# Long convolution and phase mixing on one core: reversed order of the operand blocks in SBUF, yt stores on SP, and steps, W loads and filter copies in other places

## The chip, the core and the metric

The kernel runs on one core of a Trainium2 chip, as one launch. Its time is the device time of one execution in microseconds (us). Several executions are made and the median is given. The engines are named as in the profile: PE (matmul), PEld (weight load of PE), DVE (vector engine), ACT (activation engine), POOL (GpSimd, which also issues DMAs), SP (which only issues DMAs).

## The reference

With batch 8, sequence S = 5696 and 128 channels, a causal convolution over the sequence with a filter as long as the sequence comes first, then a mixing layer over the tokens:

```python
y = irfft(rfft(x, n=2*S, axis=1) * rfft(h, n=2*S, axis=0)[None], n=2*S, axis=1)[:, :S]   # x: 8 x S x 128
theta = y @ w_theta                                  # 128 x 128
zr, zi = y * cos(theta), y * sin(theta)
v = einsum('ts,bsd->btd', w_tok_r, zr) + einsum('ts,bsd->btd', w_tok_i, zi)   # two S x S matrices
u = y + v
out = u + maximum(u @ w_ch, 0)                       # float32
```

The two S x S matrices (W below) are float32 in DRAM and most of the arithmetic is their product with zr and zi.

## The kernel before

**The convolution** is a Fourier transform made of matmuls, in eight groups: four pairs of batches (`bp`) by two halves of the channels (`dh`). Each group has four stages. `stage_a` transforms along one index of the split sequence. `stage_b` does the second transform (`f2`) and multiplies by the filter's transform, whose pieces are loaded as tiles `hs`, four of them at a time (`LEAD`); the product goes to the tile `uv_t`. `stage_c` transforms back from `uv_t` to a tile `g`, and `stage_d` from `g` to the tile `yt` with tables `e_t`. `yt` is stored to DRAM as `yt_hbm`. Stages of neighbouring groups are woven together by `woven`, which sorts their steps by a position between two bounds.

The filter's transform of the first group is taken from SBUF (`hs<-a`, line 421), and written to DRAM (`h_store`, line 369) for the other groups. `swap_rows` (lines 401 to 406) then copies it within DRAM, real and imaginary part swapped, to the second half of the rows; the loads of `hs` for the other groups (line 423) read both.

**The phase steps.** `phase_step(ti, hh)` takes 128 tokens of one half of the batches (`hh`), transposes them on PE, forms theta, sine and cosine on ACT and zr and zi on DVE in one tile `zz`, and stores y as `y2_hbm` (line 756) and `zz` as `z_hbm` (line 620) or straight into an operand block (line 616). y lies in one of six slots of 512 columns in the last three of the seven parts of block b0. `zz` is one of seven tiles taken in turn: index 0 to 3 from the pool of the `hs` tiles, 4 to 6 from a pool of its own; the counter is `zz_n`. The 22 steps of `hh` = 0 (`steps0`) need y of the first four batches. Three run ahead of the last group's stages, nine are woven into its stage c, five into its stage d, and five come behind. The 22 steps of `hh` = 1 (`steps1`) follow: two alone, twenty between the first products of the mixing (`next_steps`). Their y2 stores and half of their stores into the blocks go through POOL. Their last input, the row of the last `yt`, is copied into `ya` on POOL (line 729), and `sides["row"]` is that copy: the stores of `yt` from token H = 2816 on (line 502) are ordered behind it on POOL.

**The mixing.** The products are made for blocks of W of 3 times 64 columns, transposed by DVE (line 894), against eleven operand blocks b0 to b10 of z, each 14,336 bytes on each partition. b0 lies in the same tile as the ring of W. b1 to b6 are allocated where the convolution's tiles were, as soon as that is closed, in the order of their loads (`tile_b`, `load_b_half`); `load_b_half` loads the part that the `steps0` made from `z_hbm` and the `steps1` write the rest directly. b7 and b8 follow during `steps1`, b9 and b10 (line 817) when these are done, in a pool that lies over the tiles of `ya` and `hs`. The first stretch of products (`i == 1`) runs in four quarters `q`: halves `h` of the batches by sub-blocks `s`; the quarters with `h` = 1 need the parts that `steps1` write.

**W loads.** The W pieces are loaded on POOL with conversion to bf16, four DMAs to a piece (line 680), into a ring of six slots. `pump` issues as many as `ring["upto"]` allows and as slots are free. Before, six are released within stage c of the last group (`with_load`), two in the second quarter of the first stretch, the rest behind it. Later W pieces are released as their slots are read.

**Order.** Up to the first group's end DVE, ACT and POOL keep the order of the program text; later a scheduler orders each engine's instructions by the text and by estimated readiness, and `tc.issue_after(i)` asks that instructions on `i`'s queue come behind `i`. SP is always so scheduled. Every engine executes its instructions in order, and an instruction that waits holds up all behind it.

Of the kernel before, what the change touches and what calls it, by code (L numbers as in the profile page):

```python
# [22 lines left out]
def kernel(  # L23
# [10 lines left out]
    nc = tc.nc  # L34
# [46 lines left out]
    HD = D // 2  # L81
# [306 lines left out]
    def e_table(n):  # L388
# [9 lines left out]
            cosine(e_t[:K1, n0:n0 + 11, 0, :], k3)  # L398
        return curves

    def swap_rows():
        for c0, c1, w in ((0, NCK // 2, HD * CK), (NCK // 2, NCK - 1, HD * CK), (NCK - 1, NCK, HD * CHK[-1][1])):
            for ri in range(2):
                dst, src = (hf_hbm[c0:c1, :, r0:r0 + 64, r, :w].rearrange("c h p n -> (c h) p n")
                            for r0, r in ((64, ri), (0, 1 - ri)))
                nc.sync.dma_start(dst, src)

    def e_minus():
        nc.vector.tensor_scalar(e_neg[:K1], e_t[:K1, 1:2 * NP:2], -1.0, None, op0=mult)
# [1 line left out]
    def stage_b(a_st, dh, warm=WARM, first=False):  # L411

        hs_of = {}

        def load(c):
            if c >= NCK:
                return
            hs = hs_of[c] = fh.tile([P, 2, HD * CK], F16, tag="hs", name="hs")
            w = HD * CHK[c][1]
            for e in range(2 if first else 0):  # L420
                nc.sync.dma_start(hs[64 * e:64 * e + 64, 1, :w], hst_of(c)[64 - 64 * e:128 - 64 * e, dh])
            if not first:
                nc.sync.dma_start(hs[:, :, :w], hf_hbm[c, dh, :, :, :w])

        def chunk(c):
            c0, ck = CHK[c]
            hv = hs_of[c][:, :, :HD * ck].rearrange("p r (d k) -> p r d k", k=ck)
            straight = hst_of(c)[:, dh].rearrange("p (d k) -> p d k", k=ck).unsqueeze(1) if first else hv[:, 0:1]
            ps = f2(a_st, c, warm)
            xs = fs.tile([P, 2, HD, CK], F16, tag="xs", name="xs")  # L430
            nc.scalar.activation(xs[:, :, :, :ck], ps, AF.Copy)  # L431
            if ck == CK and not first:
                nc.vector.tensor_tensor(  # L433
                    uv[:, :, :, c0:c0 + ck],
                    xs.rearrange("p e d k -> p e (d k)").unsqueeze(1).to_broadcast([P, 2, 2, HD * CK]),
                    hv.rearrange("p r d k -> p r (d k)").unsqueeze(2).to_broadcast([P, 2, 2, HD * CK]), op=mult)
            for r in range(2 if ck < CK or first else 0):
                nc.vector.tensor_tensor(  # L438
                    uv[:, 2 * r:2 * r + 2, :, c0:c0 + ck], xs[:, :, :, :ck],
                    (hv[:, 1:2] if r else straight).to_broadcast([P, 2, HD, ck]), op=mult)  # L440
            load(c + LEAD)
        return [lambda c=c: load(c) for c in range(LEAD)], [lambda c=c: chunk(c) for c in range(NCK)]
# [35 lines left out]
    def stage_d(st, bp, dh, then=None):  # L478
        def chunk(n0, cn):
            if n0 == 0:  # L480
                st["yt"] = fy.tile([P, NB, N2], BF16, tag="yt", name="yt")
            g_, yt = st["g"], st["yt"]
            ps = psum()
            nq = 5 if cn == CN else cn
            for j in range(cn):
                o = ps[:, j // nq, (j % nq) * NB:(j % nq + 1) * NB]
                terms = terms_of(n0 + j)
                for i, (at, e_) in enumerate(terms):
                    nc.tensor.matmul(o, g_[:K1, at, :], e_, start=(i == 0), stop=(i == len(terms) - 1))
            y_out = yt[:, :, n0:n0 + cn].rearrange("p m (a q) -> p m a q", q=nq)  # L490
            y_in = ps[:, :cn // nq, :nq * NB].rearrange("p a (q m) -> p m a q", q=nq)
            if n0 in (0, 3 * CN):
                nc.vector.tensor_copy(y_out, y_in)
            else:
                nc.scalar.activation(y_out, y_in, AF.Copy)
            if n0 + cn == N2:
                if then is not None:
                    then(yt)
                for t0, t1 in [(H, S)] if then else YP:
                    for e in range(2):  # L500
                        with tc.issue_after(sides["row"]) if then else ExitStack():
                            (nc.gpsimd if then else nc.sync).dma_start(
                                yt_hbm[dh * HD:(dh + 1) * HD, 2 * bp + e, t0:t1],
                                yt[64 * e:64 * e + 64].rearrange("p m n -> p (m n)")[:, t0:t1])
        return [lambda n0=n0, cn=cn: chunk(n0, cn) for n0, cn in CHN]

    zz_n, ZB = [0], 3
    groups = [(bp, dh) for bp in range(B // 2) for dh in range(2)]

    def front(g, by_dve=(), a_=None, spare=None):  # L510
# [176 lines left out]
    sides = {"phases": None}  # L687
# [46 lines left out]
    home_of = {}  # L734
# [41 lines left out]
    for g, (bp, dh) in enumerate(groups):  # L776
# [3 lines left out]
        if last:  # L780
            for _ in range(3):
                steps0.pop(0)()
        now = ([with_load(steps0.pop(0), n < 6) for n in range(9)] if last else [], 0.0, 0.88)
        c_ = stage_c(st, last)
        if g == 0:
            ec = []
# [7 lines left out]
        if g + 2 == len(groups):  # L794
            xin.close()
            open_phases()
            load_ya0()
        now = [steps0.pop(0) for _ in range(5)] if last else []
        woven((b_, 0.0, 0.8), (stage_d(st, bp, dh, load_ya1 if last else None), 0.08 if b_ else 0.0, 1.1 if b_ else 1.0), now)
        if g + 2 == len(groups):  # L800
            load_ya1(st["yt"], True)
# [1 line left out]
    conv.close()  # L803

    bpe = [ctx.enter_context(tc.tile_pool(name="bpool_e", bufs=1, side="right", reuse_waits="tile"))]
    bts_of = {0: [], 1: []}

    def tile_b(p, j, pool):
        t_ = ring["all"][:, WB:WB + BT] if j == 0 else pool.tile([P, BT], BF16, tag=f"b{j}", name=f"b{j}")
        bt = [t_[:, k * 1024:(k + 1) * 1024].rearrange("p (r n) -> p r n", r=2) for k in range(7)]  # L810
        bts_of[p].append(bt)
        return t_

    def load_b(p, j, pool, eng=nc.scalar):
# [8 lines left out]

    def load_b_half(j):

        t_ = home_of[j] = tile_b(0, j, home_pool(j))
        for z in range(2):
            with tc.issue_after(sides["row"]) if j else ExitStack():
                d_ = nc.gpsimd.dma_start(t_[:, z * 2048:z * 2048 + 1024],
                                         z_hbm[0, j, 0, z].rearrange("i (s r) n -> (i s) (r n)", r=2)).ins  # L830
            sides["row"] = d_ if j else sides["row"]

    def sum_ops(bt):
        b11, b12, b21, b22 = (bt[q] for q in (M2, M6, M7, M5))
# [8 lines left out]
    def sum_some(n):  # L843

        for o in [o for o in owed if o[1] <= 2 or done["used"] > o[0]][:n]:
            owed.remove(o)
            o[2]()

    for j in range(7):
        load_b_half(j)  # L850
    for step in steps0:
        step()
# [273 lines left out]
    for i, (k, p, tt, j0, s0, nj) in enumerate(stretches):  # L1126
# [101 lines left out]
        if i == 1:  # L1228
            for q, (h, s) in enumerate(((0, 0), (0, 1), (1, 0), (1, 1))):
                for n in range(4):  # L1230
                    for j in range(TJ):
                        product((held, a)[s], s * TJ + j, j, n, (h,))
                        if (n * TJ + j) % 2:
                            next_steps(1)
                    if n % 2 and q == 1:
                        ring["upto"] += 1
                        pump()
                    if q == 3 and n == 0:
                        nxt = prepare(2)
# [126 lines left out]
```

## Time and profile before

| | |
|---|---|
| median of 3 executions | 2036.03 us (2028.82 to 2040.0) |
| the profiled execution | 2039.61 us, its span 2037.8 us |
| busy in the span | PE 95%, PEld 53%, DVE 75%, ACT 31%, POOL 47% |
| mean granted clock of PE | 0.985 |
| DMA through POOL's queue | 157.47 MB, 60.7% of 16 engines' time |
| DMA through SP's queue | 163.03 MB, 27.4% |
| convolution, about | 0 to 385 us |
| phase steps, about | 331 to 444 us |
| mixing, about | 394 to 2037 us |

The profile is one execution, recorded instruction by instruction. Busy time is the time in which an engine has an instruction under way; the DMA share is the busy share of the core's 16 DMA engines, and some rows of it are over 1. The granted clock is the part of PE's full clock that it ran at. Who ended a wait is inferred from the semaphores, and where several were waited for the one that came last is named. Times in the views are in us from the start of the span.

### The profile page before, as it was taken

How to read it: one execution, taken by the hardware profiler on the slowest of the kernel's cores; microseconds unless marked ns; L12 is line 12 of the kernel's file. 1: busy time of each engine (PE TensorE's matmuls, PEld its weight loads, DVE VectorE, ACT ScalarE, POOL GpSimd, SP SyncE). 2: the span in 40 equal slices, each digit the busy share in tenths (PEclk: the TensorE clock that was granted, in tenths of full speed). 3: DMA queues.
4: the chain of work that ended last, by engine and by line, in shares of the span. 5: the costliest groups of instructions: out<-in, count | busy, mean ns of one | idle time of the engine just before them, and what ended most of it. 6: DMA issues, size and time to landing. Idle time of an engine off the chain costs nothing.

```text
span 2037.8 us, 42414 instructions
## 1 busy us (share of the span) xinstructions
PE 1945.8 (95%) x16121; PEld 1079.8 (53%) x16297; DVE 1537.4 (75%) x2817; ACT 639.2 (31%) x936; POOL 964.6 (47%) x1769
## 2 busy tenths in 40 slices
PE   7799898789999999999999999999999999999998
PEld 5689897654444444444444444444444444444444
DVE  7878877557778788787867667768677786777767
ACT  6778887762232323233300000011111111111111
POOL 8324313284363545454566554553545445354450
PEclk9999999899999999999999999999999999999999
DMA  9999988899798999999999799896978879788793
GB/s 154 160 165 157 167 160 234 238 263 176 156 178 173 173 175 165 182 168 176 168 171 158 118 240 230 129 151 127 154 136 142 151 125 156 130 150 143 134 156 85
DMA packets 510349, 334.77 MB, mean 164 GB/s; under 512 B 186631, under 2 KB 463111, under 8 KB 510055
## 3 DMA queue, kind: packets, MB, share of 16 engines
q0 software_dynamic: 322368, 157.47, 60.7%
q1 hardware_dynamic: 181792, 163.03, 27.4%
q10 hardware_dynamic: 5984, 11.54, 1.6%
q8 instruction: 128, 2.10, 0.4%
q14 instruction: 77, 0.63, 0.1%
HBM read 374.82 MB, written 95.24 MB: 231 GB/s over the span
## 4 chain that ended last, share of the span: by engine, by line
PE 64%; DMA 3%; DVE 2%; POOL 2%; issue 2%; ACT 0%; DVEq 0%; ACTq 0%; POOLq 0%
PE m L1301 60%; DMA b<-z_hbm 2%; POOL ring L680 1%; DVE c L1308 1%; DMA ring<-in_moe_w_tok_r_dram 1%; PE v L981 1%; PE utp L974 1%; PE m L1305 1%; PE m L1189 1%; DVE wt L894 1%; PE theta_ps L564 0%; PE tpz L922 0%; PE m L1222 0%; POOL wl L941 0%; DMA ring<-in_moe_w_tok_i_dram 0%
## 5 line engine op out<-in xcount | busy, mean ns | idle before, releaser
L680 POOL DMA_DIRECT2D ring<-in_moe_w_tok_i_dram x720 | 387.7, 546 | 658.5 <-DVE wt L894 583.9
L680 POOL DMA_DIRECT2D ring<-in_moe_w_tok_r_dram x720 | 386.5, 547 | 135.6 <-DVE wt L894 76.5
L894 DVE STREAM_TRANSPOSE wt<-ring 128x384 f32<-128x384 f32 (+2 forms) x720 | 359.8, 524 | 109.6 <-PE m L1301 80.5
L1301 PE MATMUL m<-b,wt 128*128 128x512 bf16 x1604 | 384.6, 379 | 3.8 <-DVE wt L894 1.7
L1301 PEld LDWEIGHTS <-wt 128*128 128x128 bf16 x1804 | 176.0, 98 | 217.7 <-DVE wt L894 4.3
L1308 DVE TENSOR_TENSOR c<-c,m 128x512 f32<-128x512 f32 x412 | 266.1, 671 | 0.4 <-PE m L1301 0.4
L976 ACT ACTIVATE ring<-utp 128x512 bf16<-128x512 bf16 x85 | 50.7, 597 | 572.5 <-PE utp L974 572.5
L1222 PE MATMUL m<-b,wt 128*128 128x512 bf16 x471 | 114.6, 391 | 12.4 <-DMA b<-z_hbm 7.0
L453 PE MATMUL ps<-r_u,uv_t 128*128 128x128 f16 x1024 | 118.7, 222 | 5.1 <-DVE g__1416 L460 2.0
L971 ACT ACTIVATE ub<-c 128x512 bf16<-128x512 f32 x88 | 55.2, 628 | 200.3 <-DMA ring<-in_moe_w_tok_i_dram 116.6
L454 PE MATMUL ps<-r_v,uv_t 128*128 128x100 f16 x1024 | 116.6, 210 | 0.0
L153 POOL DMA_DIRECT2D x<-in_x_dram x128 | 99.6, 786 | 20.5 <-POOL x L151 15.0
L454 PEld LDWEIGHTS <-uv_t 128*128 128x128 f16 x1024 | 101.6, 99 | 5.8 <-issue 4.7
L453 PEld LDWEIGHTS <-uv_t 128*128 128x128 f16 x1024 | 101.7, 99 | 1.7 <-DVE uv_t L438 1.6
L433 DVE TENSOR_TENSOR uv_t<-xs,hs 128x2048 f16<-128x2048 f16 x77 | 91.2, 1222 | 12.7 <-ACT xs L431 9.1
L431 ACT ACTIVATE xs<-ps 128x1024 f16<-128x1024 f32 x96 | 90.8, 973 | 25.3 <-PE ps L270 11.6
L1222 PEld LDWEIGHTS <-wt 128*128 128x128 bf16 x528 | 51.7, 100 | 74.1 <-issue 14.0
L566 ACT ACTIVATE red<-theta_ps,magic 128x512 f32<-128x512 f32 (+1 forms) x46 | 31.6, 687 | 155.7 <-PE theta_ps L564 93.3
L270 PEld LDWEIGHTS <-w_t 64*128 64x128 f16 x3240 | 55.6, 97 | 31.2 <-issue 23.7
L924 ACT ACTIVATE ring<-tpz 128x512 bf16<-128x512 bf16 (+1 forms) x46 | 27.5, 597 | 134.4 <-PE tpz L922 120.3
L250 PE MATMUL ps<-f_t,x 89*128 89x180 f16 x512 | 64.6, 258 | 1.4 <-DVE a L257 1.3
L983 DVE SCALAR_TENSOR_TENSOR c<-v,c 128x512 f32<-128x512 f32 x88 | 60.1, 684 | 3.6 <-PE v L981 3.6
(2925 smaller groups left out, 3730.9 us busy)
## 6 DMA issues: line engine op xcount, KB each, us to landing
ring<-in_moe_w_tok_r_dram POOLq DMA_DIRECT2D x352, 96.0 KB, 4.5
ring<-in_moe_w_tok_i_dram POOLq DMA_DIRECT2D x352, 96.0 KB, 5.0
ring<-in_moe_w_tok_r_dram POOLq DMA_DIRECT2D x352, 80.0 KB, 4.5
ring<-in_moe_w_tok_i_dram POOLq DMA_DIRECT2D x352, 80.0 KB, 3.9
cp_hbm<-c SPq DMA_DIRECT2D x88, 256.0 KB, 2.6
c<-cp_hbm SPq DMA_DIRECT2D x88, 256.0 KB, 4.9
out_dram<-c SPq DMA_DIRECT2D x88, 256.0 KB, 4.8
hs<-hf_hbm SPq DMA_DIRECT2D x77, 256.0 KB, 3.7
```

Of the source, the lines that this page charges most:

```text
L153: nc.gpsimd.dma_start(x16[p0:p1, e, n0:n0 + 16, :HD], bass.AP(tensor=src.tensor, offset=src.offset + (p0 * N2 + n0) * D + dh * HD, ap=[[N2 ...
L250: nc.tensor.matmul(ps[:, i // 2, (i % 2) * 2 * K1:(i % 2 + 1) * 2 * K1], lhs(q + i), f1_t[:NB], start=True, stop=True)
L431: nc.scalar.activation(xs[:, :, :, :ck], ps, AF.Copy)
L433: nc.vector.tensor_tensor(uv[:, :, :, c0:c0 + ck], xs.rearrange("p e d k -> p e (d k)").unsqueeze(1).to_broadcast([P, 2, 2, HD * CK]), hv. ...
L453: nc.tensor.matmul(o, u_t[:, at:at + P], r_u, start=True, stop=False)
L454: nc.tensor.matmul(o[:, 2 * NP:], v_t[:, at:at + P], r_v, start=False, stop=True)
L680: nc.gpsimd.dma_start(wb[32 * i:32 * i + 32, :ng, :nj * 64], bass.AP(tensor=a.tensor, offset=a.offset + row0 * S + p * H + i * QR + j0 * 6 ...
L894: nc.vector.transpose(wt.rearrange("p j t r -> p (j t r)").bitcast(F32).rearrange("p (j g t) -> p g j t", j=TJ, g=4)[:, :ng, :nj], wb[:, : ...
L983: nc.vector.scalar_tensor_tensor(c[:m], v[:m], 0.0, c[:m], op0=ALU.max, op1=ALU.add)
L1222: nc.tensor.matmul(ms[n // 2 * 2 + h], a[n][:, j, :, r], bts_of[p][jj][n % 2 * 2 + h][:, r, :], start=(n % 2 == 0 and jj == 0 and r == 0), ...
L1301: nc.tensor.matmul(ms[q], a[q][:, j, :, r], bts[jj][q][:, r, :], start=(jj == 0 and r == 0), stop=(jj == NJ - 1 and r == 1 and q not in left))
L1308: nc.vector.tensor_tensor(c, z, ms[q], op=op)
```

## The change

- `swap_rows` orders its six copies behind the last `hs` load of the first group on SP.
- The two stores of the last `yt` from token H on go through SP instead of POOL, and are no longer ordered behind the row copies.
- The counter of the `zz` tiles starts at 4 instead of 0.
- In the last group, W loads follow four of the steps in stage c instead of six, and two of the steps in stage d; stage d has three steps instead of five.
- The tiles of the blocks b0 to b6 are allocated ahead of the loads, b0 first and then b6 down to b1. The loads of b1 and b2 are no longer ordered behind the row copies on POOL. The two steps that stage d lost come between the loads of b4 and b5.
- Two more W loads are released in the third quarter of the first products.

```diff
@@ -398,12 +398,15 @@
             cosine(e_t[:K1, n0:n0 + 11, 0, :], k3)
         return curves
 
+    hs_first = {}
+
     def swap_rows():
         for c0, c1, w in ((0, NCK // 2, HD * CK), (NCK // 2, NCK - 1, HD * CK), (NCK - 1, NCK, HD * CHK[-1][1])):
             for ri in range(2):
                 dst, src = (hf_hbm[c0:c1, :, r0:r0 + 64, r, :w].rearrange("c h p n -> (c h) p n")
                             for r0, r in ((64, ri), (0, 1 - ri)))
-                nc.sync.dma_start(dst, src)
+                with tc.issue_after(hs_first["last"]):
+                    nc.sync.dma_start(dst, src)
 
     def e_minus():
         nc.vector.tensor_scalar(e_neg[:K1], e_t[:K1, 1:2 * NP:2], -1.0, None, op0=mult)
@@ -418,7 +421,8 @@
             hs = hs_of[c] = fh.tile([P, 2, HD * CK], F16, tag="hs", name="hs")
             w = HD * CHK[c][1]
             for e in range(2 if first else 0):
-                nc.sync.dma_start(hs[64 * e:64 * e + 64, 1, :w], hst_of(c)[64 - 64 * e:128 - 64 * e, dh])
+                hs_first["last"] = nc.sync.dma_start(hs[64 * e:64 * e + 64, 1, :w],
+                                                     hst_of(c)[64 - 64 * e:128 - 64 * e, dh]).ins
             if not first:
                 nc.sync.dma_start(hs[:, :, :w], hf_hbm[c, dh, :, :, :w])
 
@@ -498,13 +502,12 @@
                     then(yt)
                 for t0, t1 in [(H, S)] if then else YP:
                     for e in range(2):
-                        with tc.issue_after(sides["row"]) if then else ExitStack():
-                            (nc.gpsimd if then else nc.sync).dma_start(
-                                yt_hbm[dh * HD:(dh + 1) * HD, 2 * bp + e, t0:t1],
-                                yt[64 * e:64 * e + 64].rearrange("p m n -> p (m n)")[:, t0:t1])
+                        nc.sync.dma_start(
+                            yt_hbm[dh * HD:(dh + 1) * HD, 2 * bp + e, t0:t1],
+                            yt[64 * e:64 * e + 64].rearrange("p m n -> p (m n)")[:, t0:t1])
         return [lambda n0=n0, cn=cn: chunk(n0, cn) for n0, cn in CHN]
 
-    zz_n, ZB = [0], 3
+    zz_n, ZB = [4], 3
     groups = [(bp, dh) for bp in range(B // 2) for dh in range(2)]
 
     def front(g, by_dve=(), a_=None, spare=None):
@@ -780,7 +783,7 @@
         if last:
             for _ in range(3):
                 steps0.pop(0)()
-        now = ([with_load(steps0.pop(0), n < 6) for n in range(9)] if last else [], 0.0, 0.88)
+        now = ([with_load(steps0.pop(0), n < 4) for n in range(9)] if last else [], 0.0, 0.88)
         c_ = stage_c(st, last)
         if g == 0:
             ec = []
@@ -795,7 +798,7 @@
             xin.close()
             open_phases()
             load_ya0()
-        now = [steps0.pop(0) for _ in range(5)] if last else []
+        now = [with_load(steps0.pop(0), n < 2) for n in range(3)] if last else []
         woven((b_, 0.0, 0.8), (stage_d(st, bp, dh, load_ya1 if last else None), 0.08 if b_ else 0.0, 1.1 if b_ else 1.0), now)
         if g + 2 == len(groups):
             load_ya1(st["yt"], True)
@@ -803,12 +806,12 @@
     conv.close()
 
     bpe = [ctx.enter_context(tc.tile_pool(name="bpool_e", bufs=1, side="right", reuse_waits="tile"))]
-    bts_of = {0: [], 1: []}
+    bts_of = {0: {}, 1: {}}
 
     def tile_b(p, j, pool):
         t_ = ring["all"][:, WB:WB + BT] if j == 0 else pool.tile([P, BT], BF16, tag=f"b{j}", name=f"b{j}")
         bt = [t_[:, k * 1024:(k + 1) * 1024].rearrange("p (r n) -> p r n", r=2) for k in range(7)]
-        bts_of[p].append(bt)
+        bts_of[p][j] = bt
         return t_
 
     def load_b(p, j, pool, eng=nc.scalar):
@@ -823,12 +826,14 @@
 
     def load_b_half(j):
 
-        t_ = home_of[j] = tile_b(0, j, home_pool(j))
+        if j not in home_of:
+            home_of[j] = tile_b(0, j, home_pool(j))
+        t_ = home_of[j]
         for z in range(2):
-            with tc.issue_after(sides["row"]) if j else ExitStack():
+            with tc.issue_after(sides["row"]) if j > 2 else ExitStack():
                 d_ = nc.gpsimd.dma_start(t_[:, z * 2048:z * 2048 + 1024],
                                          z_hbm[0, j, 0, z].rearrange("i (s r) n -> (i s) (r n)", r=2)).ins
-            sides["row"] = d_ if j else sides["row"]
+            sides["row"] = d_ if j > 2 else sides["row"]
 
     def sum_ops(bt):
         b11, b12, b21, b22 = (bt[q] for q in (M2, M6, M7, M5))
@@ -846,7 +851,11 @@
             owed.remove(o)
             o[2]()
 
+    for j in (0, 6, 5, 4, 3, 2, 1):
+        home_of[j] = tile_b(0, j, home_pool(j))
     for j in range(7):
+        while j == 5 and len(steps0) > 5:
+            steps0.pop(0)()
         load_b_half(j)
     for step in steps0:
         step()
@@ -1232,7 +1241,7 @@
                         product((held, a)[s], s * TJ + j, j, n, (h,))
                         if (n * TJ + j) % 2:
                             next_steps(1)
-                    if n % 2 and q == 1:
+                    if n % 2 and q in (1, 2):
                         ring["upto"] += 1
                         pump()
                     if q == 3 and n == 0:
```

## The prediction

> **What bounds the kernel now.** I read the page first, then busy time by stage, then the waits and the timelines of the stages that are not full. The stages, by the windows view (stretch, its length, then busy PE, PEld, DVE, ACT, POOL with counts, then granted clock, DMA share, GB/s):
>
> ```profile
> PE 1945.8 (95%) x16121; PEld 1079.8 (53%) x16297; DVE 1537.4 (75%) x2817; ACT 639.2 (31%) x936; POOL 964.6 (47%) x1769
> ...
> 330.00:368.00 38.00, 29.44 (x455) 25.79 (x458) 24.38 (x48) 30.42 (x48) 15.19 (x32) 0.96 1.08 270
> 368.00:385.00 17.00, 16.34 (x275) 14.74 (x279) 8.15 (x17) 11.56 (x19) 0.64 (x2) 0.90 0.59 141
> 385.00:394.00 9.00, 6.44 (x78) 4.86 (x77) 7.45 (x20) 8.94 (x17) 1.48 (x3) 1.00 0.91 231
> 394.00:404.00 10.00, 5.36 (x29) 2.88 (x28) 5.51 (x13) 5.61 (x10) 6.43 (x12) 0.66 0.93 291
> 404.00:440.00 36.00, 35.39 (x327) 22.95 (x332) 21.20 (x54) 33.49 (x56) 30.25 (x56) 1.00 1.00 291
> 440.00:480.00 40.00, 33.16 (x146) 14.50 (x148) 25.05 (x48) 4.65 (x9) 25.41 (x47) 0.91 1.04 230
> 480.00:600.00 120.00, 115.71 (x590) 54.83 (x601) 92.50 (x185) 39.42 (x64) 53.72 (x101) 1.00 0.86 158
> 600.00:1170.00 570.00, 566.37 (x2819) 266.86 (x2874) 443.36 (x898) 140.63 (x227) 302.62 (x556) 1.00 0.94 167
> ```
>
> From 600 us on PE is busy 99% of the time and this change touches nothing there; what comes earlier at 600 comes earlier at the end. The change acts at 50 to 70 us (filter copies) and in the handover from convolution to mixing, 330 to 480, where PE idles 22.7 us (the sum of its gaps over 0.2 us). Four places matter. In the waits and timelines (start, length, engine, line, operation; in brackets the idle time before it and what ended it):
>
> ```profile
> 52.43 0.90 SPq L406 DMA_DIRECT2D hf_hbm<-hf_hbm  x1
> 53.44 11.56 SPq L421 DMA_DIRECT2D hs<-a__241  x16
> 58.87 0.69 DVE L438 TENSOR_TENSOR uv_t<-xs,hs 128x1024 f16<-128x1024 f16 x1 [3.93 <-DMA hs<-a__241]
> ...
> DVE ring L754 <- DMA y_hbm<-ring: 6.8, 5, 2.0
> ...
> 384.37 1.06 POOL L729 DMA_DIRECT2D ya<-yt  x2 [22.01 <-ACT yt L495]
> 385.41 1.06 POOL L502 DMA_DIRECT2D yt_hbm<-yt  x2
> 395.61 3.76 POOL L829 DMA_DIRECT2D b<-z_hbm  x7 [9.13 <-DMA z_hbm<-zz]
> 398.98 1.01 PE L1222 MATMUL m<-b,wt 128*128 128x512 bf16 x2 [4.64 <-DMA b<-z_hbm]
> ...
> 448.38 1.06 POOL L616 DMA_DIRECT2D b<-zz  x2
> 455.29 7.05 PE L1222 MATMUL m<-b,wt 128*128 128x512 bf16 x25 [4.34 <-DMA b<-zz]
> 464.40 1.59 PE L1222 MATMUL m<-ring,wt 128*128 128x512 bf16 x4 [2.06 <-DVE wt L894]
> ```
>
> (1) One swap copy stands on SP ahead of the hs loads of the first group, and DVE waits 3.93 us for the first of them. (2) In 330 to 368 the DMA share is 1.08 with six W loads, and DVE waits for y2 stores. (3) POOL stands at the b1 load until 395.61, PE until 398.98. (4) At 451 PE waits for the last step's b<-zz stores, which POOL issued at 448.4 to 449.4, 4.6 us or more after DVE had made that zz (443.8).
>
> **What holds b1.** The timeline puts the 9.13 us down to z stores, but j=1 needs steps 1 to 8 alone, stored long before. The rows fit another cause: the yt stores of L502, issued at 385.41 and 385.93, land after 7.5 to 8.9 us (the source view of L502), thus at about 394.8. Sizes in the code say the same: six blocks of 14.3 KB take 86 KB of what the convolution leaves, in order uv_t (46.3 KB), tables (to 63.9), xs (to 68.1), yt (to 79.4), g. The outermost block covers 71.7 to 86.0 KB, yt and g; that b1 waits for yt makes b1 the outermost. Reversed, b6 lies there, b5 over tables, xs and yt, b4 over uv_t's end and tables, and b1 to b3 over uv_t alone, which is free when the last stage c ends (about 366).
>
> **The change part by part**, in us gained:
>
> Swap copies behind all 24 hs loads. The first late load goes out at 52.43 instead of 53.44, its twin 0.55 later; landing takes 2.9 in the median and 4.6 at most (source view of L421), so DVE goes on at 55.9 to 57.6 instead of 58.87: 1.3 to 3.0. DVE and ACT run almost without gaps behind it, so it reaches the end. I take 2.3. Behind the six copies on SP stand the next group's hs loads; they first went out at 73.85, are used at 92.19 and land within 6.6, so about 11.7 of slack covers the 0.9 of one more copy there. Without that cover it would cost 0.9.
>
> Two W loads move out of the last stage c (four left) into stage d, where the DMA share is 0.59. Two PE gaps of 1.76 and 2.93 at 350 and 357 lie behind y2 stores that land late in the W traffic: bounds 0 and 4.7. I take 2.0, nearer the lower end, because ACT is at 30.42 of 38 there and can't shed more than its 7.6 of idle time. POOL idles 22.01 before 384.37, which hides the 4.3 of issue time of two loads; the last yt row load stands behind them. If it were not hidden, the row load would come up to 4.3 late.
>
> Reversed blocks, with b1 and b2 no longer ordered behind the row loads. Their loads can go out in POOL's 22 us of idle time; b3 and b4 follow the row loads at 382 to 384; b5 and b6 come two steps later. The 4.64 goes. So does most of the slow time after it: from 398.98 to 403.47 PE did six products and one step, which at the later pace (four products and a step per 1.96, a product 0.216) take 2.4 instead of 4.5, so 2.1. Bounds 0 and 6.7; I take 6.0, since the trace names the wait. The Trainium skill ("TensorE: Matmul & The Clock Gate", Part 1) says that after an idle window of some 3.4 us the array runs at half clock until it has been busy about as long again; by it the slow part would be 1.7, not 2.1, and the term's upper end 6.3. The trace has clock 0.66 in that stretch.
>
> Two phase steps fewer in stage d (three, not five), two more behind the b4 load. Same ACT work, three activations 1.65 apart per step (385.76 to 391.79 in ACT's timeline), and ACT is busy 8.94 of 9 in 385 to 394: nothing gained, 0. yt is done about 3 earlier, which helps the row loads; ACT stays the next limit up to 394.
>
> yt stores on SP. POOL loses 1.06 of issue, SP gains about 1.2. The stores for t over H are read much later; b5 and b6 wait for them. Who stands behind them on SP: z and y2 stores of the last steps of the first half. 0 as long as six y slots cover (second rival).
>
> Rotation of zz starts at 4, and W loads 9 and 10 go out in the third quarter of the first products instead of behind them. Block b10's load left SP at 455.79, 10.6 after b9's; it waits for the last steps' zz slots, which the new start moves out of its region (44 steps modulo 7: the last three zz then lie in the other pool). Two W loads that were issued from 449.44 to 457.30 now come earlier, and POOL starts its stores earlier, since eight of twelve b loads have left 395 to 404. Against this, eight W issues stand in front of the last b<-zz. What there is to win: 4.34 and 2.06 of gaps, and slow matmuls (25 in 7.05 instead of 5.4, and 20 from 464.40 to 470.42 instead of 4.3), 9.8 in all. What there is to lose: the two loads at their slow rate, 7.9, less 4.3 at the undisturbed rate that POOL's earlier start pays for, 3.6. I take 2.3.
>
> Sum: 2.3 + 2.0 + 6.0 + 2.3 = 12.6. The profiled execution took 2039.6 (span 2037.8 and 1.8 around it), 3.6 above the median of 2036.0; it would become 2027.0, and the median 2023.4.
>
> **Rivals.** First: POOL's queue sets the end of the steps. It was busy 30.25 of 36 from 404 to 440 and still behind at 449. If it stays behind, 449.4 doesn't move, its 5.8 of idle time takes part of the two W loads' 7.9, and 2.1 come on top, while what was gained before 440 is lost except the swap: 2036.0 - 2.3 + 2.1 = 2035.8. Against it: 4.3 of b issues leave its queue. Chance 0.17.
>
> Second, slower: the yt stores hold SP up. z and y2 stores are issued in SP's order; y has six slots, and at 1.65 a step they cover 9.9. One after the other the two stores took 8.2 and 8.9, so if SP's stores stand behind both, 17.1, ACT loses 7.2, b5, b6 and all behind them on POOL wait as well, and the gains in the handover are gone: 2036.0 - 2.3 + 7.2 = 2040.9; it decides once SP lags by over 9.9. For it: SP's y2 store at 385.52 took 1.92 and a z store at 388.16 2.41 while these stores ran on POOL. Against: they then ran side by side within 9. Chance 0.13. Beside this, the Trainium skill ("DMA: Bandwidth & Descriptors", Queues, rings and completion order) says that a DMA engine alternates between queues but takes one queue's descriptors in order; by that rule the move would do what this rival says. No run shown here has such stores on SP with the steps' stores behind them.
>
> Third: the edit doesn't do what it says, b1 being held by z stores as the timeline has it, or the order within the pool not following the order of making. Then 6.0 are missing: 2029.4. Chance 0.10.
>
> **How the numbers follow.** The forecast has 0.60. Its own range is 2014 to 2029. About 0.5%, 10.2 us, is what can be told from no change here. Of the 0.60, 0.52 lie under 2025.9; of the first rival 0.14 lie within the bound, 0.02 over and 0.01 under; of the second 0.05 within, 0.08 over; of the third 0.02 under, 0.06 within, 0.02 over. Sum: faster 0.55, same 0.33, slower 0.12. The range goes from all terms at their best (3.0 + 4.7 + 6.7 + 9.8 = 24.2, so 2011.8, taken as 2012) to the second rival with a little above it, 2042.
>
> **What would show it.** Right: on SP no L406 row before the last L421 row, and DVE's wait at 59 under 2; b1 and b2 loads on POOL before the row loads (L729), and no PE wait for b<-z_hbm near 394; b10's load within 3 of b9's; the 451 gap not longer than 4.3. At a fixed mark, PE's steady run of L1301 starts some 12 earlier. Wrong: b1 still waiting for yt, DVE or ACT waiting over 5 for y2 stores in 385 to 394, or the gap before the last b<-zz at 8 or more.

## The result, and the profile after

| | before | after |
|---|---|---|
| median | 2035.43 us (2028.82 to 2040.0, 15 runs) | 2042.74 us (2039.48 to 2056.91, 15 runs) |
| ratio after / before | | 1.0049, 95% interval 1.0036 to 1.0062 |
| the profiled execution, its span | 2039.61, 2037.8 | 2056.91, 2055.1 |

The change makes the kernel slower by 7 us (medians) to 10 us (ratio). The profiled execution after was the slowest of its fifteen, 14 above their median: three groups of its convolution took 41 us each against 36 to 37, and from 110 to 330 us the granted clock was 0.89 against 0.97. Places behind the convolution are therefore read from the end of the seventh `yt`, at 332.5 before and 345.4 after. In the second profile of this kernel (run e1) it is at 339.4. Source lines from 401 on have moved down by 2 to 9.

The page's first part, then the windows, cut at the same distances from the seventh `yt` as those shown of before (13 us later); columns as there:

```profile
PE 1970.8 (96%) x16297; PEld 1097.4 (53%) x16297; DVE 1536.9 (75%) x2817; ACT 640.1 (31%) x936; POOL 967.7 (47%) x1767
...
343.00:381.00 38.00, 30.20 (x459) 26.07 (x456) 24.94 (x48) 30.30 (x48) 13.80 (x28) 0.96 1.06 266
381.00:398.00 17.00, 16.91 (x282) 15.08 (x283) 7.91 (x17) 11.05 (x18) 4.91 (x11) 0.90 0.59 132
398.00:407.00 9.00, 3.92 (x45) 2.77 (x43) 4.49 (x12) 7.42 (x14) 1.96 (x4) 0.97 1.00 317
407.00:417.00 10.00, 2.86 (x19) 2.11 (x19) 3.90 (x10) 2.97 (x5) 2.67 (x5) 0.50 0.87 284
417.00:453.00 36.00, 36.00 (x318) 22.78 (x317) 22.54 (x57) 33.19 (x55) 28.99 (x53) 0.96 0.98 263
453.00:493.00 40.00, 32.49 (x172) 15.36 (x171) 25.89 (x52) 9.93 (x17) 24.55 (x46) 0.91 0.99 221
```

Stage c is as it was (PE 30.20 for 29.44 of 38, DMA share 1.06 for 1.08). Stage d ends earlier, but the 19 us behind it hold 6.78 of PE's work where they held 11.80. The later stretches are level with before.

Timelines of that place (start, length, engine, line, operation; in brackets the idle time before it and what ended it), SP, POOL, DVE, ACT and PE in turn:

```profile
394.67 0.54 SPq L759 DMA_DIRECT2D y_hbm<-ring  x1
395.30 0.47 SPq L505 DMA_DIRECT2D yt_hbm<-yt  x1
396.50 3.15 SPq L623 DMA_DIRECT2D z_hbm<-zz  x2
399.71 1.76 SPq L505 DMA_DIRECT2D yt_hbm<-yt  x1
401.52 0.71 SPq L759 DMA_DIRECT2D y_hbm<-ring  x1
...
395.64 3.24 POOL L834 DMA_DIRECT2D b<-z_hbm  x6
399.57 0.54 POOL L834 DMA_DIRECT2D b<-z_hbm  x1 [0.68 <-DMA ya<-yt]
403.19 0.54 POOL L834 DMA_DIRECT2D b<-z_hbm  x1 [3.08 <-DMA ya<-yt]
412.05 2.12 POOL L834 DMA_DIRECT2D b<-z_hbm  x4 [8.32 <-DMA z_hbm<-zz]
...
411.09 0.42 DVE L757 COPY ring<-ps 128x512 bf16<-128x512 bf16 x1 [7.00 <-DMA y_hbm<-ring]
...
411.61 0.69 ACT L592 ACTIVATE sin<-ps,zero_b 128x512 f16<-128x512 f32 x1 [6.19 <-DVE ring L757]
...
414.14 0.59 PE L752 MATMUL tpz<-ident_bf,ya 128*128 128x128 bf16 x4 [11.23 <-ACT cos L595]
```

The last `yt` ended at 394.2. The y2 store of a y made at 395.19 to 395.61 went out only at 401.52, behind both `yt` stores and two z stores, and by the semaphore events of the trace it landed at 411.07. DVE needs its slot six copies later and stands 7.00 us, ACT 6.19, PE 11.23. The first product begins at 418.36, 73.0 after the seventh `yt`; before it was 61.2.

And PE at the end of the first products:

```profile
471.16 1.02 PE L1231 MATMUL m<-b,wt 128*128 128x512 bf16 x4 [1.84 <-DMA b<-z_hbm]
475.88 5.28 PE L1231 MATMUL m<-b,wt 128*128 128x512 bf16 x12 [3.70 <-DMA b<-z_hbm]
...
488.65 0.59 PE L1276 MATMUL m<-yy,ident_bf 128*128 128x512 bf16 x2 [1.43 <-DMA yy<-y_hbm]
```

The 4.34 for b<-zz and the 2.06 for wt are gone; waits for b9, b10 and the addends (yy) have come. The Strassen products are the steady run of products behind the first ones (L1301 before, L1310 after). The stretch from the seventh `yt` to the first of them took 180.3 before, 185.8 after and 185.0 in e1. What follows takes 1521 to 1525 in every profile.

### The profile page after: what moved, and what is told of

The parts are those of the page before. It is cut to its first block, busy times and chain, and to the rows that moved or that the text cites. A ratio compares the mean times of both kernels' runs of the same rounds, so it can differ in the third digit from the quotient of the medians.

```text
span 2055.1 us, 42580 instructions
## 1 busy us (share of the span) xinstructions
PE 1970.8 (96%) x16297; PEld 1097.4 (53%) x16297; DVE 1536.9 (75%) x2817; ACT 640.1 (31%) x936; POOL 967.7 (47%) x1767
## 4 chain that ended last, share of the span: by engine, by line
PE 65%; DMA 4%; DVE 2%; issue 1%; POOL 1%; ACT 0%; DVEq 0%; ACTq 0%; POOLq 0%
PE m L1310 61%; DMA ring<-in_moe_w_tok_i_dram 3%; DVE c L1317 1%; PE v L990 1%; POOL ring L683 1%; PE utp L983 1%; PE m L1314 1%; DMA ring<-in_moe_w_tok_r_dram 1%; DVE wt L903 0%; PE theta_ps L567 0%; PE tpz L931 0%; PE m L1198 0%; DMA wl<-in_moe_w_tok_i_dram 0%; DVE b L840 0%; DVE c L992 0%
## 5 line engine op out<-in xcount | busy, mean ns | idle before, releaser
L1310 PE MATMUL m<-b,wt 128*128 128x512 bf16 x1640 | 388.3, 379 | 1.9 <-DVE wt L903 1.7
L1310 PEld LDWEIGHTS <-wt 128*128 128x128 bf16 x1804 | 176.0, 98 | 217.5 <-DVE wt L903 4.3
```

What stands on the lines that cost most here:

```text
L1310: nc.tensor.matmul(ms[q], a[q][:, j, :, r], bts[jj][q][:, r, :], start=(jj == 0 and r == 0), stop=(jj == NJ - 1 and r == 1 and q not in left))
```

## The experiments

Each result is the median in us, then in brackets the ratio to the kernel before, run on the same chip, with its 95% interval. Three marks of each profile are used: **A**, from the seventh `yt`'s end to the 22nd `zz` (the first half's steps); **C**, from the last `zz` to the first Strassen product; and **lag**, how long after the last `zz` POOL issues the last b<-zz store. Before: A 62.3, C 69.0, lag 5.2. After: A 69.2, C 69.1, lag 5.1.

**e1_again.** No edit: the changed kernel once more.

> The changed kernel once more, because its profiled execution took 2056.9 us, 14 above its median, with groups 3 to 5 of the convolution at 41 us each against 36 before. If that is a disturbance of one execution, the eight ends of yt now lie within 1 us of those before up to the seventh (332.5) and the last some 3 earlier (381). Theory A (yt stores on SP): DVE again waits 5 to 8 us for a y2 store some 15 us after the last yt's end, and the first product comes about 11 late in spite of the earlier yt. Rival (the groups themselves became slower): the ends of yt are late again. Time 2040 to 2045 under both.

2043.78 (1.0044, 1.0024 to 1.0065). The stall is there again: DVE 6.82 for a y2 store, A 67.9. The seventh `yt` ends at 339.4, still later than 332.5; how much of that is the swap copies' doing stays open to the end.

**e2_yt_pool.** The yt stores as before:

```diff
-                        nc.sync.dma_start(
+                        with tc.issue_after(sides["row"]) if then else ExitStack():
+                            (nc.gpsimd if then else nc.sync).dma_start(
```

> The changed kernel with the two last yt stores back on POOL behind the row copies. Theory A (SP's stores of the last steps stand behind the yt stores and land late, 7.0 us of DVE's wait and about 2 of slow clock behind it): the wait for the y2 store falls under 2, the first product comes 7 to 9 earlier, 2033 to 2037 us. Rival B (the loads of b0 to b4, which no longer wait for yt, crowd the stores of the last steps whoever issues the yt stores): the wait stays at 5 to 8, 2041 to 2045. Rival C (the two steps behind the b4 load are simply late): no change either, 2041 to 2045.

A falls to 61.3, so theory A has the stall right. But the time is 2045.11 (1.0052, 1.0032 to 1.0072): nothing gained. Its lag is 13.2. The profiled execution was the fastest of the twelve (2037.88), and its stretch from the seventh `yt` to the Strassen products, 177.9, is no longer than before's.

**e3_five_steps.** Five steps in stage d again (and none between b4 and b5):

```diff
-        now = [with_load(steps0.pop(0), n < 2) for n in range(3)] if last else []
+        now = [with_load(steps0.pop(0), n < 2) for n in range(5)] if last else []
```

> The changed kernel with five steps in the last stage d again and none between the loads of b4 and b5. Theory A: the yt stores are still on SP, with fewer steps behind them, so the stall shrinks but does not go: gains 1 to 4, 2038 to 2042. Rival B: the loads still go out at yt's end into fewer open steps, 2 to 5 gained. Rival C (the two steps behind b4 are late and everything waits for their z): the end of the first half's steps comes 5 or more earlier, 2033 to 2037.

2040.67 (1.0031, 1.0009 to 1.0053). A 62.8: with fewer steps behind the yt stores the stall is gone from A; one wait of 5.4 for a y2 store is left behind the 22nd `zz`. Lag 10.7.

**e4_blocks_up.** Rising order, b1 and b2 behind the rows again:

```diff
-    for j in (0, 6, 5, 4, 3, 2, 1):
+    for j in (0, 1, 2, 3, 4, 5, 6):
-            with tc.issue_after(sides["row"]) if j > 2 else ExitStack():
+            with tc.issue_after(sides["row"]) if j else ExitStack():
```

> The changed kernel with b0 to b6 allocated in rising order and b1 and b2 ordered behind the row copies again; two steps still behind the b4 load, yt stores still on SP. Theory A: the stall stays and b1 waits for yt's readers again, which now are on SP and late: 2043 to 2050. Rival B: the block loads go out later, the last steps' stores land in time, the stall goes: 2034 to 2038. Rival C: no change, 2041 to 2045.

2041.17 (1.0033, 1.0014 to 1.0051). A 61.9, lag 12.1. So each of three edits takes the stall of 7 out of A, and none brings the time back: theory A is half the answer.

**e5_no_swap.** Swap copies where they were:

```diff
-                with tc.issue_after(hs_first["last"]):
-                    nc.sync.dma_start(dst, src)
+                nc.sync.dma_start(dst, src)
```

> The changed kernel with the filter's swap copies where they were (free to go ahead of the second half of the first hs loads). All five profiles with the copies behind those loads show PE gaps of 2.0 to 2.9 us at about 101 (a wait for hs<-hf_hbm) and at about 173 us, with a granted clock of 0.5 behind them, and the seventh yt ends at 336.4 to 345.4; before shows gaps of 1.0 and 1.5 there, full clock, and 332.5. Theory D (the later copies cost in the convolution what they gain at 59 us and more): the gaps fall under 1.6, the seventh yt ends at 330 to 335, and the time falls by 4 to 8, to 2035 to 2039; the handover's stall of some 7 stays. Rival E (convolutions differ by chance between executions, and the copies gain their 2.3): the gaps stay or come at random, 2043 to 2047.

2042.52 (1.0036, 1.0020 to 1.0052). Theory D fails. PE's gap at 101 is gone, but the one at 173 is still 2.6, so that one isn't theirs, and the time is no better.

**e6_only_swaps.** The same lines put into the kernel before, and nothing else (the edit of e5 reversed).

> The kernel before with the swap copies behind all hs loads of the first group, and nothing else. The prediction's step: 2.3 gained, 2032 to 2035. Theory D: the gaps at 101 and 173 come back, 2 to 8 lost, 2038 to 2044. Rival E: as the step, and the seventh yt's end is not later than 334.

2037.19 (1.0010, 0.9993 to 1.0027). No gain, and no clear loss.

**e7_no_swap_no_yt.** The edits of e2 and e5 together.

> The changed kernel with both the swap copies and the yt stores as before; the reversed blocks, the two later steps, the W loads and the zz rotation remain. Theories A and D together: the convolution of before and the shorter handover (the steps of the first half end 1 earlier relative to the seventh yt, steady products 2 earlier), 2030 to 2036. Rival E: 2040 to 2045, like the run with the yt stores alone put back.

2040.80 (1.0030, 1.0012 to 1.0048): a miss for A and D together. Lag 11.3, C 71.4.

**e8_only_blocks.** The kernel before with the reversed blocks alone:

```diff
+    for j in (0, 6, 5, 4, 3, 2, 1):
+        home_of[j] = tile_b(0, j, home_pool(j))
-            with tc.issue_after(sides["row"]) if j else ExitStack():
+            with tc.issue_after(sides["row"]) if j > 2 else ExitStack():
```

> The kernel before with b0 to b6 allocated in reverse and the b1 and b2 loads not ordered behind the row copies; nothing else. The prediction's step: b1 no longer waits for yt, the 4.64 of PE's wait and about 2 of slow clock go, 2029 to 2032. Rival B (the wait only moves: the loads go out earlier, and z stores of the last steps or the row copies hold b3 to b5 instead): PE's first product comes earlier but the steady products at the same time, 2034 to 2038. The convolution is that of before, so its seventh yt's end is another sample of the 332.5.

2035.81 (1.0002, 0.9984 to 1.0019): nothing gained. PE's first b1 product in the timeline, and two rows of the waits of 385 to 445 (us in total, times, longest):

```profile
394.03 0.59 PE L1226 MATMUL m<-b,wt 128*128 128x512 bf16 x2 [1.07 <-DMA b<-z_hbm]
...
DVE zz L602 <- DMA z_hbm<-zz: 8.8, 4, 3.1
...
ACT sin L589 <- DVE zz L602: 3.9, 1, 3.9
```

The 4.64 shrank to 1.07, and DVE now waits 8.8 for z stores, which run beside the earlier block loads; that these slow them is likely, not shown. The eleventh product matmul came 67.6 after the seventh `yt` (72.5 before), the last `zz` 112.0 after it (111.3 before). The last `zz` came no earlier.

**e9_no_rot.** The zz counter from 0:

```diff
-    zz_n, ZB = [4], 3
+    zz_n, ZB = [0], 3
```

> The changed kernel with the zz counter starting at 0 again. In all profiles with the rotation SP issues the addends' loads (yy) some 18 us after b9's load, against 2 without it, PE then waits 1.4 to 3.5 for yy, and before that 3.4 to 4.3 for b9 or b10. Theory F (the rotation only moves the wait for the last zz slots from b10 to the addends): the yy loads come 2 us after b9's again, PE's wait for yy goes, b10's load comes some 10 after b9's; from the last zz to the Strassen part 66 to 67 instead of 69 to 70; 2039 to 2041. Rival G (the W loads in the third quarter crowd b9, b10 and yy): the order is restored but the waits for b9 or b10 stay, 2041 to 2045.

2041.73 (1.0048, 1.0029 to 1.0067). A 70.2, C 66.8. The yy loads came 12.6 after the last `zz`, not 3; PE waited 4.38 behind W loads instead.

**e10_no_quarter.** Third quarter without W loads:

```diff
-                    if n % 2 and q in (1, 2):
+                    if n % 2 and q == 1:
```

> The changed kernel with two W loads released in the second quarter only, the rest behind the first products as before. Theory G: b9's and b10's loads land within 6, PE's wait for them falls under 1, and a wait for b<-zz or wt of 2 to 4 takes its place, since the W loads are then issued 7 us later: 2039 to 2042. Theory F: the wait for yy stays at 1.4 to 3.5, 2041 to 2045.

2041.70 (1.0033, 1.0015 to 1.0052). C 66.2, lag 0.8; the waits for b9 and b10 are gone, one of 3.74 for yy remains, A is 68.9.

**e11_yt_rot_q.** The edits of e2, e9 and e10 together.

> The changed kernel with three parts undone: yt stores on POOL, zz counter from 0, no W loads in the third quarter. What remains: the swap copies, the reversed blocks, two steps behind b4, two W loads in stage d. If theory A (stall of 7 by the yt stores on SP) and theory F or G (2 to 3 at b9, b10 and yy) account for the loss, it is within 2 of before: 2033 to 2037. If the two later steps or the W loads in stage d are the cause (rival C), it stays at 2040 to 2045.

2033.95 (0.9998, 0.9981 to 1.0015): the whole loss is gone. A 60.9, C 66.0, lag 3.8. The cause is among these three parts.

**e12_only_yt.** The kernel before with the yt stores on SP alone (the edit of e2 reversed).

> The kernel before with only the last two yt stores on SP. Theory A: the y2 and z stores of the last five steps stand behind them; a wait for a y2 store of 3 to 7 us at the end of the first half's steps, 2037 to 2043. The prediction's step: no change, 2034 to 2037.

2033.78 (1.0007, 0.9986 to 1.0028): alone the move costs nothing. A row of POOL's timeline, the b1 load:

```profile
391.26 4.82 POOL L828 DMA_DIRECT2D b<-z_hbm  x9 [10.68 <-DMA yt_hbm<-yt]
```

Here the trace names the yt stores as what holds b1. The block loads go out only from 391.26 on, and DVE waits 1.3 for a y2 store. On SP the order is that of the profile after:

```profile
380.68 1.92 SPq L501 DMA_DIRECT2D yt_hbm<-yt  x1
382.70 3.90 SPq L619 DMA_DIRECT2D z_hbm<-zz  x2
386.65 0.80 SPq L501 DMA_DIRECT2D yt_hbm<-yt  x1
387.49 0.58 SPq L755 DMA_DIRECT2D y_hbm<-ring  x1
```

This y2 store went out 6.9 after its y was made (380.19 to 380.61), later than the 5.9 of the profile after. But by the semaphore events it landed 3.55 later, not 9.55, and no block load was under way beside it, where after had eight issued from 395.64 to 403.19.

**e13_rot_left** (the edits of e2 and e10), **e14_quarter_left** (of e2 and e9) and **e15_best** (of e2, e5, e9 and e10).

> The changed kernel with the yt stores on POOL and no W loads in the third quarter, but the zz counter still from 4. Against the run with all three undone (2034) it has the rotation alone. Theory F (the rotation moves the wait for the last zz slots to the addends): the yy loads come late, PE waits 2 to 4 for yy, 2036 to 2040. Theory G (the W loads in the third quarter do the harm): 2033 to 2036. Theory H (only both together, because an early b10 and early W loads crowd each other): 2033 to 2037.

> The changed kernel with the yt stores on POOL and the zz counter from 0, but W loads in the third quarter. Theory G: b9's load lands after 7 to 10 and the last b<-zz late, 2037 to 2041. Theory F: 2033 to 2036. Theory H: 2033 to 2037.

> The changed kernel with four parts undone: yt stores on POOL, zz counter from 0, no W loads in the third quarter, swap copies where they were. What remains of the change: reversed blocks, two steps behind the b4 load, two W loads in stage d. The profile with three undone had the shortest stretch from the seventh yt to the Strassen part (174.8 us against 180.3, 178.0 and 178.5 in kernels near the one before), and the swap copies seem to cost 2 in the convolution: 2029 to 2033. If the copies cost nothing: 2033 to 2036.

e13: 2037.15 (1.0022, 1.0005 to 1.0038), lag 2.2. e14: 2042.82 (1.0054, 1.0032 to 1.0076), lag 11.0. e15: 2033.21 (1.0002, 0.9983 to 1.0021): level with before. No version found beats it. POOL's timeline of e14 up to the last b<-zz (last `zz` at 450.3), and PE behind it:

```profile
452.11 0.55 POOL L620 DMA_DIRECT2D b<-zz  x1 [1.43 <-DMA ring<-in_moe_w_tok_r_dram]
452.64 0.59 POOL L760 DMA_DIRECT2D y_hbm<-ring  x1
453.29 0.54 POOL L620 DMA_DIRECT2D b<-zz  x1
453.82 2.20 POOL L684 DMA_DIRECT2D ring<-in_moe_w_tok_i_dram  x4
455.99 0.59 POOL L760 DMA_DIRECT2D y_hbm<-ring  x1
457.52 0.56 POOL L620 DMA_DIRECT2D b<-zz  x1 [0.93 <-DMA b<-zz]
459.02 0.53 POOL L620 DMA_DIRECT2D b<-zz  x1 [0.95 <-DMA y_hbm<-ring]
459.69 0.59 POOL L760 DMA_DIRECT2D y_hbm<-ring  x1
460.76 1.06 POOL L620 DMA_DIRECT2D b<-zz  x2 [0.48 <-issue]
...
464.44 7.50 PE L1232 MATMUL m<-b,wt 128*128 128x512 bf16 x26 [6.00 <-DMA b<-zz]
```

The same of e11 (last `zz` at 446.6):

```profile
448.21 1.07 POOL L620 DMA_DIRECT2D b<-zz  x2
449.27 0.59 POOL L760 DMA_DIRECT2D y_hbm<-ring  x1
449.86 1.06 POOL L620 DMA_DIRECT2D b<-zz  x2
...
456.36 5.77 PE L1232 MATMUL m<-b,wt 128*128 128x512 bf16 x26 [1.56 <-DMA b<-zz]
```

Of the eight W issues of the third quarter four stand in these rows and four went out at 446.28 to 447.92, all among the last steps' stores. The store at 452.11 waits for the first of those W DMAs to land, and the stores issued from 448.45 to 457.52 landed after 4.3 to 6.6 us; in e11 those of 443.63 to 447.63 took 2.8 to 3.8, and only the last five, beside the W DMAs that follow them, 5.0 to 6.4.

**e16_only_rot_q.** The kernel before with two edits (those of e9 and e10 reversed):

```diff
-    zz_n, ZB = [0], 3
+    zz_n, ZB = [4], 3
-                    if n % 2 and q == 1:
+                    if n % 2 and q in (1, 2):
```

> The kernel before with the zz counter from 4 and W loads in the third quarter, nothing else. The prediction's step: 2.3 gained, 2031 to 2034. Theories F, G and H: b10's load follows b9's within 3, PE waits 3 to 4 for b9 or b10 and 1 to 4 for yy, from the last zz to the Strassen part 69 to 71; 2 to 6 lost, 2037 to 2041.

2038.13 (1.0026, 1.0006 to 1.0045), lag 10.6, yy 19.0 after the last `zz`, and a wait of 3.71 for b10.

**e17_yt_left** (the changed kernel with the edits of e9 and e10) and **e18_only_quarter** (the kernel before with the second edit of e16 alone).

> The changed kernel with the zz counter from 0 and no W loads in the third quarter; the yt stores stay on SP. This completes the eight combinations of those three parts. Theory K (two causes that hide behind each other: the yt stores on SP stall the first half's steps by 7, the early W loads put eight POOL issues in front of the last b<-zz and send it out 11 us after the last zz instead of 4; with both, the stall lets POOL catch up, so that either one alone costs nearly as much as both): the stall of 6 to 8 is there, the last b<-zz goes out within 5 of the last zz, 2037 to 2042. Against it: 2033 to 2036, the stall being paid back before the Strassen part.

> The kernel before with two more W loads in the third quarter of the first products, nothing else. Theory K: sixteen W issues instead of four to eight between 425 us and the last b<-zz, which goes out 9 to 13 after the last zz; PE's gap before it 4 to 7; 2038 to 2044. The prediction's step (POOL is ahead by then and the early loads are gained): 2032 to 2035.

e17: 2039.11 (1.0025, 1.0012 to 1.0038): A 69.6, DVE's wait 7.5, lag 0.8, and C only 61.8. The stall is paid back in part, not in full. e18: 2040.02 (1.0034, 1.0020 to 1.0049), lag 11.5, and in PE's timeline:

```profile
461.13 8.41 PE L1222 MATMUL m<-b,wt 128*128 128x512 bf16 x26 [7.09 <-DMA b<-zz]
```

Two W loads in another place, alone, cost this kernel 0.34%, about 7 us. The stretch of this one profile is 182.6, 2.3 longer than before's, so most of the 7 isn't seen in it. The eight combinations, in kernels that keep the rest of the change:

| yt stores | zz from | W in third quarter | ratio | A | C | lag |
|---|---|---|---|---|---|---|
| POOL | 0 | no (e11) | 0.9998 | 60.9 | 66.0 | 3.8 |
| POOL | 4 | no (e13) | 1.0022 | 63.9 | 65.1 | 2.2 |
| POOL | 0 | yes (e14) | 1.0054 | 64.7 | 69.3 | 11.0 |
| POOL | 4 | yes (e2) | 1.0052 | 61.3 | 68.5 | 13.2 |
| SP | 0 | no (e17) | 1.0025 | 69.6 | 61.8 | 0.8 |
| SP | 4 | no (e10) | 1.0033 | 68.9 | 66.2 | 0.8 |
| SP | 0 | yes (e9) | 1.0048 | 70.2 | 66.8 | 4.4 |
| SP | 4 | yes (after) | 1.0049 | 69.2 | 69.1 | 5.1 |

The costs don't add: the stall alone costs 0.27%, the early W loads alone 0.56%, both (e9) 0.50%. Where the stall delays the steps, the lag falls from 11.0 to 4.4: POOL has time to catch up. Take away the stall and the lag is back. That is the account of e2's ratio, though its one profile doesn't show the loss.

Two things stay open. The zz start alone (e13 against e11) costs 0.24%, with intervals that overlap and 3.0 more in A; chance isn't excluded. And of the 11 us between e14 and e11 their profiles show 8.8 in the stretch from the seventh `yt`: 3.3 are in C, behind the late stores, but 3.8 in A, ahead of the moved loads. How much the lag costs by itself isn't settled.

## Why the prediction was wrong

The prediction said 2023.4 and faster; it is 2042.7. Its second rival had the stall, but the dearest part was another. Step by step:

**W loads in the third quarter and the zz start: +2.3 forecast. The step that failed most.** By themselves the loads cost about 7 (e18), with the zz start 5 (e16). The prediction priced the eight issues at 7.9 and set 4.3 of an earlier start of POOL against it, which left 3.6 to lose, and it took a gain within those bounds. The 7.9 was about right: the lag is 11.0 (e14) and 11.5 (e18) against 3.8 and 5.2, and PE's gap 7.09 against 4.34. The credit was the mistake. The earlier block loads brought little of the 4.3, if any (lag 4.2 in e8 and 3.8 in e11 with them, 5.2 before and 4.3 in e6 without), and e14 has them and lags by 11.0 all the same: POOL's issues wait for earlier DMAs to land, and behind the W DMAs these land late. The prediction's own mark, a gap of 8 or more, was nearly met in e18; in the profile after, the stall hides it. The zz start did what was forecast (b10's load 1.7 after b9's, 12.0 to 3.1 after the last `zz`). But PE had not waited for b10 before, and in the kernels that have both edits the yy loads slipped from 3 to 18 or more after the last `zz`.

**yt stores on SP: 0 forecast.** The runs have a stall of 7.00 on DVE, near the second rival's 7.2, and a slow clock behind it. It needs company: alone the move costs nothing (e12), and the old block order (e4) or five steps in stage d (e3) takes the stall out of A. The step that failed is to have weighed the six y slots with before's five steps in stage d and before's quiet POOL. The change itself put two more steps behind `yt` and let eight block loads out beside their stores.

That the rival's price came out is partly luck. It set 17.1, both stores one after the other, against 9.9 of cover. Measured are 15.5 (5.9 until the y2 store went out, 9.55 until it landed) against 8.5 until DVE wanted the slot. The larger part is the y2 store's own landing time, which the rival didn't have; in e12 it was 3.55.

The prediction also said that no run shown had yt stores on SP with the steps' stores behind them. The profile before has them, for the seventh `yt`:

```profile
332.53 6.38 SPq L502 DMA_DIRECT2D yt_hbm<-yt  x8
...
340.75 0.41 SPq L756 DMA_DIRECT2D y_hbm<-ring  x1
...
349.79 0.42 DVE L754 COPY ring<-ps 128x512 bf16<-128x512 bf16 x1 [1.97 <-DMA y_hbm<-ring]
```

The y2 store of 340.75 landed at 349.76, 9.0 later, and DVE stood for it; it is one of the late y2 stores that the prediction put down to the W traffic. Which of the two made it late isn't shown.

**Reversed blocks: 6.0 forecast, nothing measured (e8).** That b1 waited for the yt stores was right (e12 names them), and PE's wait shrank to 1.07. Two steps failed. The loads of b1 and b2 were to go out in POOL's idle time ahead of the row copies; in e8, as in the profile after, POOL has the row copies first:

```profile
381.40 1.06 POOL L729 DMA_DIRECT2D ya<-yt  x2 [20.76 <-ACT yt L495]
382.44 1.06 POOL L502 DMA_DIRECT2D yt_hbm<-yt  x2
383.50 2.70 POOL L831 DMA_DIRECT2D b<-z_hbm  x5
```

And the end of PE's wait was to come through; but products and steps alternate there, and the steps' last `zz` did not move (112.0 for 111.3).

**Swap copies: 2.3 forecast, no gain found.** On SP the first late hs load went out at 50.83 instead of 53.44, no copy stands ahead of the last of them, and the first stage b ended at 65.2 instead of 67.6, 2.4 earlier. By the end of the next one (108.3 against 108.5) it was lost. SP's timeline, then DVE's:

```profile
50.83 12.35 SPq L424 DMA_DIRECT2D hs<-a__241  x16
63.22 11.28 SPq L409 DMA_DIRECT2D hf_hbm<-hf_hbm  x6
...
100.88 3.60 DVE L437 TENSOR_TENSOR uv_t<-xs,hs 128x2048 f16<-128x2048 f16 x3 [2.33 <-DMA hs<-hf_hbm]
```

In the twelve profiles with this edit that wait is 1.1 to 3.5 in all, in the eight without it 0.4 to 1.3. The slack of 11.7 that the prediction took as cover belonged to the first four loads only. What DVE waits for is a later one. Four pairs that differ in this edit alone (e6 and before, after and e5, e2 and e7, e11 and e15) differ by 0.10, 0.13, 0.22 and -0.04%: no gain; the mean is a loss of 2 us, which no single pair settles.

**Two W loads out of stage c: 2.0 forecast, 0 found.** Stage c took 35.5 from the seventh `yt` before and after. The text moves two loads of four DMAs, but in the order that ran, 22 of the 24 W DMAs still went out by 366.76, and only the last two at 388.83 and 393.93.

**Two steps fewer in stage d: 0 forecast.** `yt` did end 2.8 earlier, as said; the two steps pay for it behind b4, inside the stall.

The sums roughly agree: near the kernel before, the stretch from the seventh `yt` to the Strassen products took 176.6 to 180.3 (before, e6, e8, e12; mean 178.4), in the changed kernel 185.0 and 185.8, 7 more. What follows takes the same, so the 2 or 3 that the ratio has beyond that should lie ahead of it: the swap edit's profiles have the seventh `yt` at 332.8 to 345.4 (mean 338), the others at 328.2 to 338.6 (mean 333). How much of that is the edit's and how much chance stays open.

## What to carry to other kernels

A DMA moved to an earlier place can delay every later issue of its queue. Where a queue keeps a fixed number under way, as POOL's did here, price the move by the landing time of the moved transfer, not only by its issue time. A wait that an edit removes may be what kept two streams of transfers apart; ask whose stores now run beside the freed loads before its length is booked as gain. When one cause hides another, undoing either alone may show nothing: undo them in all combinations before a theory is dropped.

## What the runs showed of the hardware

POOL never had more than eight of its DMAs under way here. In four profiles (before, after, e11, e14) none of its some 1,670 issues each began earlier than 0.28 us after the landing of the one eight issues before it, and 404 to 463 of them began within 0.7 of it. In e14 the W DMAs of 446.28, 446.84 and 447.37 landed at 451.5, 451.8 and 452.7; the three stores eight issues later went out at 452.11, 452.64 and 453.29. Whether the kernel's semaphores (POOL's DMAs use eight in turn) or the chip set this limit was not tried. SP's DMAs use eight in turn as well, and in the stall its issues of 406.51, 408.16, 409.72 and 411.09 began 0.02 to 0.06 after the eighth before each had landed. For that of 409.72 the eighth before is the second `yt` store.

In the stall PE stood idle for 11.23 us up to 414.14, and the granted clock was 0.50 in 407 to 417. The Trainium skill ("TensorE: Matmul & The Clock Gate", Part 1) says that the array goes to half clock after an idle window of some 3.4 us and leaves it after at least one busy window of that length. The first half agrees with this 0.50. That one busy window is enough does not hold everywhere: in the profile after, a gap of 2.6 at 172, shorter than the window, was followed by a clock of 0.50 from 176 to 190, with PE busy throughout; in e1, behind the same gap, it ended at 184.

The Trainium skill ("DMA: Bandwidth & Descriptors", Queues, rings and completion order) has one queue's descriptors taken in order and different queues alternating. By that rule alone yt stores on SP would cost wherever steps' stores follow them; e12 has them there at 1.0007. So here the rule says what can collide; whether it costs went with the load beside it (landing in 9.55 us after, 3.55 in e12).
